# The first batch's attention product in plain float32, in a fused attention, SoLU and Mish kernel on one core

## The chip, the cores and the metric

The kernel runs on one core of a Trainium2 chip. The metric is the device time of one execution in microseconds (us). The kernel before was run three times; one more number counts here, the span of the profiled execution, which is the time from its first to its last instruction.

## What is computed

The reference is an attention block followed by two feed-forward blocks over 2304 tokens. It is cut here to what matters.

```python
# x: (4, 8, 512, 64), state: (4, 8, 32, 64), all float32
a     = softmax(x @ state^T / sqrt(64));   xread = a @ state      # 512 tokens per batch
a2    = softmax(state @ x^T / sqrt(64));   sread = a2 @ x         # 32 tokens per batch
t     = concat(xread, sread)  ->  (2304, 512)
h     = t @ w_in                                  # 512 x 1024
solu  = h * softmax(h)
ln    = (solu - mean) / sqrt(var + 1e-6) * g_ln
y     = ln @ w_out                                # 1024 x 512
h2    = y @ w2_in                                 # 512 x 2048
out   = (h2 * tanh(softplus(h2))) @ w2_out        # 2048 x 512
```

## The kernel before

**Stages.** The 2304 tokens lie in 17 tiles of 128 rows: four tiles for each batch's 512 tokens and one tile for the state tokens of all batches. The first stage makes the attention weights, the hidden layer `h` of each tile, its SoLU and layer norm, and the product with the first output matrix. The second stage runs over three passes of 6, 6 and 5 tiles and multiplies with the second block's matrices by a scheme with seven products in place of eight (the products are on line 860, their sums on lines 871 to 882, the activation on lines 894 and 901). Pass 0 also splits and stores the second block's weights, which passes 1 and 2 fetch again.

**Attention merged with the first matrix.** The kernel doesn't form `xread`. It multiplies the state with `w_in` first (lines 493 and 504), which gives merged weights `sw` with 128 rows (four heads of 32 states) for each half `q` of the heads, and then `h` of a tile is the transposed attention weights `aT` times `sw`, summed over the two halves (line 530, `s_a0`).

**Split products.** A factor is kept as a rounded part `hi` in the type F32R and a rest `lo`, and one product is three matmuls: hi*hi, hi*lo and lo*hi. For the attention weights `weights_of` makes the two parts (ScalarE casts on line 346, VectorE subtracts on line 348), for the merged weights `split_sw` does (lines 486 and 488). A flag per batch, `A`, takes another way through the same functions, which the kernel before has off for all four batches:

```python
def weights_of(b, q, src):
    both = aTp.tile([P, 2, S], F32R, tag="aT", name="aT")
    if eng('A', b, False, True):
        (nc.scalar.copy if eng('C', 2 * b + q, ...) else nc.vector.tensor_copy)(out=f32(both[:, 0]), in_=src)
        aT[b, q] = f32(both[:, 0]); return
    hi, lo = both[:, 0], both[:, 1]
    nc.scalar.copy(out=hi, in_=src)                                             # line 346
    nc.vector.tensor_tensor(out=lo, in0=src, in1=f32(hi), op=ALU.subtract)      # line 348

def s_a0(i):
    for q in range(2):
        terms = ((aT[b, q], f32(sw(b)[0])),) if eng('A', b, False, True) \
                else ((ah, wh), (ah, wl), (al, wh))
        for k, (a_, w_) in enumerate(terms):
            for hf in range(2):                                                 # two halves of 512 columns
                nc.tensor.matmul(out=ph[:, hf*512:(hf+1)*512], lhsT=a_[:, c*P:(c+1)*P],
                                 rhs=w_[:, q, hf*512:(hf+1)*512], ...)          # line 530
```

**A tile's chain.** After `s_a0` the steps of `s_a1` follow: VectorE takes the maximum (line 539), ScalarE the exponential (542), VectorE the product with `h` (544), ScalarE the squares (548), GpSimd some small steps, and ScalarE or VectorE the norm (559 or 562). The accumulator `ph` of a tile is a PSUM tile of a pool with two slots, which the products for `sw` use too. Its last reader is line 548. So tile k+2 can't start before line 548 of tile k has run. Then the normed tile is transposed on TensorE (575) or by VectorE and DMA (586 to 595), split in two parts (579 and 581, or 597 and 599), and multiplied with the output matrix (616).

**What sets the order.** The order of issue on all engines is one table, `ORDER`: each two letters name a step of the program, and every naming issues the step's next piece. Strings of flags, `FLAGS`, choose the engine for single operations: `M` for the copy on line 871 and `S` for that on line 921 (ScalarE or VectorE), `P` for the subtraction on line 599 (VectorE or GpSimd), `B`, `W` and `T` for the steps that make float32 out of the 64-bit inputs (lines 149 to 165), `N`, `Q` and `Z` for small ones. Each engine runs its own instructions in the order of issue.

Of the kernel before, what the change touches and what calls it, by code (L numbers as in the profile page):

```python
# [19 lines left out]
B, H, S, NS, D = 4, 8, 512, 32, 64  # L20
DM, FF1, FF2 = 512, 1024, 2048
NTOK = B * (S + NS)
P = 128
# [48 lines left out]
    "AAAABGBGATBIBIBKBKAUAUARARAWAWBABAA0A0BHBHA-A-ATBHBHA6A6BJABABBJBPAQAQBJBOANANAYAYBLBJAJAJA2A2BLBCBCBPADADAaAaBO"  # L72
    "BRAFAFBQBRBXA8A8BBBLBBBUBBAVAVBLBXBXA1APAPBTAXAXA1BQA1BUBBA4A4AOAOBTBSAZAZA_A_BeA7A_A7BSBUBEBEA1A7BhBhA_AbAbA3Bg"
    "BgBDBDASASB5BDBeBeA7B5AcAcBUBUA3B5B7AeAeA9BDB6B7AgAgB5B7BVBiBiB6B7B8A3AiAiBVB6A5A9A5A9A5BbBbAdAdA3BVBYBYA9AfAfA5"
    "B8BfBfBFBFBaBaBVBjBZBZBFB5BjB8BVBVBVBnAhAhB6BcB7AjAjBFB6BWB6B8BdBcBWBkBkBnBWBMBqBnBdAkAkBlB8AmAmB_BNCJAoAoBdBoAq"
# [1131 lines left out]
```

## Time and profile before

| | |
|---|---|
| median of 3 runs (lowest to highest) | 576.29 us (575.89 to 576.59) |
| the profiled execution's own time | 576.29 us |
| its span | 574.6 us |
| TensorE (PE) busy | 558.4 us (97%) |
| VectorE (DVE) busy | 500.2 us (87%) |
| ScalarE (ACT) busy | 364.2 us (63%) |
| GpSimd (POOL) busy | 54.5 us (9%) |
| granted TensorE clock | 1.000 of 2.4 GHz |

The profiled execution took the median's time, and 1.7 us of it lie outside the span. Busy time is a share of the whole span; the stages differ, so the rows further down are read by stretch. A PE row's duration runs on after the next matmul has begun, so the price of a matmul is the distance from its start to the next one's start.

### The profile page before, as it was taken

To read this page: it belongs to the slowest core of one execution; us is meant where nothing else is said; L and a number is where in the kernel's file an instruction comes from. 1 tells how busy PE (TensorE), PEld (TensorE's weight loads), DVE (VectorE), ACT (ScalarE), POOL (GpSimd) and SP (SyncE) were. 2 spreads that over 40 slices of the span, in tenths; PEclk is the share of its full clock that TensorE was granted. 3 is DMA by queue.
4 is the path that set the end of the run, shared out by engine and by line. 5 is a ranking of instruction groups with operands and counts; after the bars stand their busy time and mean duration, and the time that the engine had idled before them with its cause. 6 is when DMAs were issued, how large, how long until landed. Compare 5 with 4: busy or idle time off the path is not lost. (4 is left out here: it accounts for less than half of the span.)

```text
span 574.6 us, 9808 instructions
## 1 busy us (share of the span) xinstructions
PE 558.4 (97%) x3557; PEld 497.6 (87%) x3557; DVE 500.2 (87%) x949; ACT 364.2 (63%) x659; POOL 54.5 (9%) x134
## 2 busy tenths in 40 slices
PE   9977999999999999999999999999999999999997
PEld 3435787899789998888988989999999999999996
DVE  5999988896668878999999996689889998889996
ACT  5997968656458956999998774542433636433340
POOL 0102212210023000000000000000000024000024
PEclk9999999999999999999999999999999999999999
DMA  8952205123206688899988699876866779888832
GB/s 345 414 200 94 74 38 165 57 75 111 74 38 220 204 292 277 307 348 391 342 312 292 249 337 320 312 264 231 327 204 250 255 263 333 302 293 332 293 144 92
DMA packets 47279, 136.04 MB, mean 237 GB/s; under 512 B 5376, under 2 KB 20864, under 8 KB 46720
## 3 DMA queue, kind: packets, MB, share of 16 engines
q1 hardware_dynamic: 47232, 135.42, 66.3%
q8 instruction: 28, 0.46, 0.3%
q14 instruction: 19, 0.16, 0.1%
HBM read 96.60 MB, written 38.80 MB: 236 GB/s over the span
## 5 line engine op out<-in xcount | busy, mean ns | idle before, releaser
L860 PE MATMUL hp<-xo,w2r 128*128 128x384 f32 (+1 forms) x504 | 94.3, 328 | 0.1
L860 PEld LDWEIGHTS hp<-xo,w2r 128*128 128x128 f32 x504 | 84.8, 188 | 3.1 <-DVE u L874 0.4
L860 PE MATMUL hp<-xo,w2swh 128*128 128x384 f32 (+1 forms) x336 | 83.3, 331 | 2.0 <-DVE c L882 0.5
L616 PE MATMUL pm<-ln_l,gw_hi 128*128 128x256 f32 (+1 forms) x256 | 77.6, 303 | 0.6 <-ACT raw_c L621 0.5
L616 PE MATMUL pm<-ln_h,gw_hi 128*128 128x256 f32 (+1 forms) x256 | 74.9, 293 | 0.0
L616 PE MATMUL pm<-ln_h,gw_lo 128*128 128x256 f32 (+1 forms) x256 | 74.5, 291 | 0.0
L972 DVE TENSOR_TENSOR acc<-po,acc 128x384 f32<-128x384 f32 (+1 forms) x136 | 68.4, 521 | 3.6 <-PE po L967 3.1
L860 PEld LDWEIGHTS hp<-xo,w2swh 128*128 128x128 f32 x336 | 59.1, 188 | 6.2 <-DVE c L882 1.6
L901 ACT ACTIVATE gh<-c 128x384 fp32r<-128x384 f32 (+1 forms) x57 | 29.2, 519 | 53.2 <-DVE c L882 47.8
L860 PE MATMUL hp<-xo,w2swl 128*128 128x384 f32 (+1 forms) x168 | 55.0, 328 | 0.0
L616 PEld LDWEIGHTS pm<-ln_l,gw_hi 128*128 128x128 f32 x256 | 48.3, 189 | 4.5 <-DVE ln_l L581 1.1
L939 ACT CAST qh<-t 128x384 fp32r<-128x384 f32 (+1 forms) x60 | 28.4, 489 | 35.6 <-DVE t L931 18.0
L882 DVE TENSOR_TENSOR c<-hp,u 128x384 f32<-128x384 f32 (+1 forms) x72 | 38.0, 532 | 13.4 <-PE hp L860 12.9
L616 PEld LDWEIGHTS pm<-ln_h,gw_hi 128*128 128x128 f32 x256 | 48.2, 188 | 1.2 <-issue 0.7
L616 PEld LDWEIGHTS pm<-ln_h,gw_lo 128*128 128x128 f32 x256 | 48.6, 190 | 0.0
L530 PE MATMUL ph<-swh,aT 128*128 128x512 f32 x128 | 40.5, 405 | 3.8 <-ACT ph L548 2.5
L965 PE MATMUL po<-ql,w2oh 128*128 128x384 f32 (+1 forms) x120 | 39.5, 330 | 0.2 <-DVE acc L972 0.2
L966 PE MATMUL po<-qh,w2oh 128*128 128x384 f32 (+1 forms) x120 | 38.8, 324 | 0.0
L967 PE MATMUL po<-qh,w2ol 128*128 128x384 f32 (+1 forms) x120 | 38.8, 323 | 0.0
L159 ACT CAST w<-w 128x512 f16<-128x512 f32 x22 | 30.7, 1394 | 3.2 <-DVE w L156 2.8
L941 DVE TENSOR_TENSOR ql<-t,qh 128x384 fp32r<-128x384 f32 (+1 forms) x60 | 30.9, 533 | 1.1 <-ACT qh L939 0.6
L860 PEld LDWEIGHTS hp<-xo,w2swl 128*128 128x128 f32 x168 | 31.5, 188 | 0.0
(454 smaller groups left out, 1355.2 us busy)
## 6 DMA issues: line engine op xcount, KB each, us to landing
w2r<-ki SPq DMA_DIRECT2D x16, 768.0 KB, 6.1
w2ol<-ko SPq DMA_DIRECT2D x15, 768.0 KB, 6.3
w2oh<-ko SPq DMA_DIRECT2D x15, 768.0 KB, 6.0
w<-in_w2i SPq DMA_DIRECT2D x16, 512.0 KB, 5.4
w2swl<-ki SPq DMA_DIRECT2D x8, 896.0 KB, 6.7
w2swh<-ki SPq DMA_DIRECT2D x8, 896.0 KB, 7.5
w<-in_w2o SPq DMA_DIRECT2D x12, 512.0 KB, 5.5
ki<-w2r SPq DMA_DIRECT2D x8, 768.0 KB, 8.8
```

What stands on the lines that cost most here:

```text
L159: nc.scalar.copy(out=src.bitcast(F16)[..., 1], in_=f32(high))
L530: nc.tensor.matmul(out=ph[:, hf * 512:(hf + 1) * 512], lhsT=a_[:, c * P:(c + 1) * P], rhs=w_[:, q, hf * 512:(hf + 1) * 512], start=q == 0 ...
L616: nc.tensor.matmul(out=pm[:, :n], lhsT=w_[:, k, m * P:(m + 1) * P], rhs=l_[:, c0:c0 + 4 * len(blk), k, :], start=k == 0 and j == 0, stop=k ...
L860: nc.tensor.matmul(out=r, lhsT=w_[:, 0, k * P:(k + 1) * P], rhs=x_[:, k, :n], start=s in (0, 1, 3, 4) and cnt == 0, stop=cnt == 5, skip_gr ...
L882: nc.vector.tensor_tensor(out=c, in0=bank[ps, fp, s], in1=u, op=ALU.add)
L901: nc.scalar.activation(out=gh, in_=src, func=AF.Mish)
L939: nc.scalar.copy(out=hi, in_=src)
L941: on('V', ((ps - 1) * NFP + fp) * 4 + int(name[1]) - 1).tensor_tensor(out=lo, in0=src, in1=f32(hi), op=ALU.subtract)
L965: nc.tensor.matmul(out=r, lhsT=wh[:, a, c], rhs=x[1], start=first or not held, stop=False)
L966: nc.tensor.matmul(out=r, lhsT=wh[:, a, c], rhs=x[0], start=False, stop=False)
L967: nc.tensor.matmul(out=r, lhsT=wl[:, a, c], rhs=x[0], start=False, stop=last or not held)
L972: on.tensor_tensor(out=o, in0=x, in1=y, op=ALU.add)
```

## The change

It turns flag `A` on for batch 0, so that its attention weights and merged weights are kept in plain float32 in one part each, and each product of its four tiles is one plain matmul in place of three. `C` puts the two copies of the attention weights on ScalarE and those of the merged weights (a new line in the profile, 483) on VectorE. `ORDER` is a new table, and flags of other steps change with it. No function changes.

```diff
 FLAGS = dict(
-    A="0000",
-    B="0000011100011000010010111010",
-    C="000000000000",
+    A="1000",
+    B="0000111100011000010110111101",
+    C="110000000000",
...
-    M="001100001110000000000010",
-    N="00010001110010001",
+    M="001001111010000000010100",
+    N="01000010100101001",
-    P="00000000000000000",
-    Q="111011111111110101010001",
+    P="00000100000000000",
+    Q="111110101100110101010001",
-    S="000110",
+    S="111001",
-    W="1101010100000001111000000000",
-    X="00111010001100100101010001000101",
+    W="1101010100000011111010000000",
+    X="10101000101110010000110001010001",
-    Z="11101011110011101",
+    Z="11100101011001100",
...
-    "P2QGP3QFQHQFPzP4QJQGQHQGP0QIQHQKQIQIQJQKQJQK"
+    "QHQFP0P4QGQIQHQGPzQHQJQIQKQIQJQKQJQK"
```

Over the whole program the instructions that change in number are: on PE line 530 from 192 matmuls to 160 (48 split ones less, 16 plain ones more); on DVE line 348 from 8 to 6, line 488 from 8 to 6, line 483 from 0 to 2, line 599 from 9 to 8 (one goes to POOL), line 871 from 6 to 8, line 921 from 2 to 4; on ACT line 346 from 8 to 6, line 341 from 0 to 2, line 486 from 8 to 6, line 871 from 18 to 16, line 921 from 4 to 2; and a few of the short steps on lines 149 to 165 and 422 to 546 go from one engine to another.

The first place is PE from the first tile of batch 0 to the second. In the names, `ph` with the lowest number is tile 0's accumulator, the next one tile 1's; `aT` are the attention weights of the two halves, `swh` and `swl` the merged weights, and the `tr` rows are transposes for batch 1's and batch 0's softmax. Before:

```order
L465 MATMUL tr_477<-ident_58,srs_436 128x128
L530 MATMUL ph_484<-swh_389,aT_444 128x512 x2
L530 MATMUL ph_484<-swl_390,aT_444 128x512 x2
L530 MATMUL ph_484<-swh_389,aT_444 128x512 x2
L334 MATMUL tr_501<-ident_58,tt_475 128x128 x4
L530 MATMUL ph_484<-swh_389,aT_471 128x512 x2
L530 MATMUL ph_484<-swl_390,aT_471 128x512 x2
L530 MATMUL ph_484<-swh_389,aT_471 128x512 x2
L334 MATMUL tr_523<-ident_58,tt_494 128x128 x4
L530 MATMUL ph_530<-swh_389,aT_444 128x512 x2
```

And now:

```order
L465 MATMUL tr_473<-ident_58,srs_455 128x128
L530 MATMUL ph_475<-swh_404,aT_427 128x512 x2
L334 MATMUL tr_495<-ident_58,tt_484 128x128 x4
L530 MATMUL ph_475<-swh_404,aT_469 128x512 x2
L334 MATMUL tr_515<-ident_58,e2_506 128x128 x4
L530 MATMUL ph_520<-swh_404,aT_427 128x512 x2
L334 MATMUL tr_532<-ident_58,tt_488 128x128 x4
L530 MATMUL ph_520<-swh_404,aT_469 128x512 x2
L334 MATMUL tr_546<-ident_58,e2_511 128x128 x4
L334 MATMUL tr_552<-ident_58,tt_484 128x128 x4
```

Each half of a tile is now one pair of matmuls, and the transpose for batch 1's other half (`tt_494` before, `tt_488` now) stands behind the first half of tile 1, no longer ahead of tile 1.

The second place is DVE ahead of the first tile's maximum (line 539). `swl_457` before and `swl_442` now are batch 1's merged weights, whose second products `ph_461` and `ph_446` hold the slot that tile 1 needs. Before:

```order
L488 TENSOR_TENSOR swl_390<-ph_370,swh_389 128x1024
L348 TENSOR_TENSOR aT_444<-tr_428,aT_444 128x512
L488 TENSOR_TENSOR swl_457<-ph_408,swh_456 128x2x512
L420 TENSOR_REDUCE m2_481<-st_447 128x1
L348 TENSOR_TENSOR aT_471<-tr_438,aT_471 128x512
L420 TENSOR_REDUCE m2_499<-st_446 128x1
L295 SCALAR_TENSOR_TENSOR gw_lo_131<-wo64_291,g_t_59,gw_hi_130 128x512 x2
L385 TENSOR_REDUCE mx_520<-tr_501 128x16
L488 TENSOR_TENSOR swl_457<-ph_461,swh_456 128x2x512
```

And now:

```order
L483 COPY swh_404<-ph_371 128x1024
L431 RECIPROCAL s2_354<-s2_354 128x1
L295 SCALAR_TENSOR_TENSOR gw_lo_131<-wo64_279,g_t_59,gw_hi_130 128x512
L488 TENSOR_TENSOR swl_442<-ph_416,swh_441 128x2x512
L295 SCALAR_TENSOR_TENSOR gw_lo_131<-wo64_279,g_t_59,gw_hi_130 128x512
L420 TENSOR_REDUCE m2_482<-st_460 128x1
L420 TENSOR_REDUCE m2_490<-st_459 128x1
L488 TENSOR_TENSOR swl_442<-ph_446,swh_441 128x2x512
L385 TENSOR_REDUCE mx_509<-tr_495 128x16
```

The subtractions for `aT` are gone, a copy stands in the place of the subtraction for `sw`, and batch 1's second subtraction has moved ahead of line 385.

The third place is ACT from the transposed weights of batch 1 to tile 0's squares (line 548). Now:

```order
L438 COPY a2_526<-tr_515 128x512
L542 ACTIVATE ez_530,lnsm_523<-ph_475,lnsm_523 128x1024
L389 ACTIVATE tt_488<-tt_488 128x512
L346 CAST aT_567<-tr_552 128x512
L548 ACTIVATE ph_475,lnsm_523<-ez_530,lnsm_523 128x1024
```

This piece reads the same before with other numbers: line 548 of tile 0 stands behind line 346, and line 346 waits for a transpose that PE runs, now as before, behind all of tile 1.

## Rows read from the trace of the kernel before

**Rows 1.** Windows view: stretch, length, busy us of each engine, TensorE clock, DMA share, GB/s.

```profile
core 0: us, PE busy (x) PEld busy (x) DVE busy (x) ACT busy (x) POOL busy (x), PEclk, DMA share, GB/s
40.00:50.00 10.00, 8.70 (x57) 6.44 (x57) 9.86 (x17) 7.45 (x17) 1.07 (x3) 1.00 0.33 108
50.00:60.00 10.00, 6.95 (x74) 4.61 (x59) 9.93 (x16) 8.38 (x15) 4.50 (x17) 1.00 0.31 105
60.00:70.00 10.00, 9.59 (x96) 7.07 (x94) 9.92 (x21) 9.94 (x19) 2.70 (x10) 1.00 0.34 107
70.00:110.00 40.00, 40.00 (x357) 32.36 (x350) 34.10 (x47) 27.81 (x47) 8.88 (x28) 1.00 0.27 93
202.00:330.00 128.00, 125.93 (x640) 112.93 (x639) 120.03 (x256) 110.25 (x189) 0.00 (x0) 1.00 0.87 311
330.00:571.00 241.00, 240.71 (x1453) 234.81 (x1451) 210.56 (x440) 107.42 (x241) 19.95 (x20) 1.00 0.76 270
```

**Rows 2.** Timeline of PE, 40 to 68 us: start, us, instruction, idle time before it and releaser.

```profile
40.97 0.73 PE L530 MATMUL ph<-swh,aT 128*128 128x512 f32 x2 [0.38 <-DVE swl L488]
...
45.81 0.73 PE L530 MATMUL ph<-swh,aT 128*128 128x512 f32 x2 [0.92 <-DVE swl L488]
...
53.45 0.73 PE L530 MATMUL ph<-swh,aT 128*128 128x512 f32 x2 [2.06 <-ACT ph L548]
...
58.09 0.65 PE L452 MATMUL sr<-xn_t,a 128*32 128x64 f32 x32 [0.82 <-DVE tt L381]
...
59.71 1.07 PE L530 MATMUL ph<-swh,aT 128*128 128x512 f32 x4
60.62 0.62 PE L530 MATMUL ph<-swl,aT 128*128 128x512 f32 x2
...
63.70 0.73 PE L530 MATMUL ph<-swh,aT 128*128 128x512 f32 x2 [0.41 <-ACT ph L548]
...
67.56 0.37 PE L616 MATMUL pm<-ln_l,gw_hi 128*128 128x256 f32 x1
```

**Rows 3.** Timeline of PE at the plain float32 products of the state tile.

```profile
156.14 2.74 PE L517 MATMUL ph<-w_in_t,xs 128*128 128x512 f32 x6
158.71 1.02 PE L517 MATMUL ph<-w_in,xs 128*128 128x512 f32 x2
159.17 0.68 PE L616 MATMUL pm<-ln_l,gw_hi 128*128 128x256 f32 x1
159.69 0.28 PE L616 MATMUL pm<-ln_h,gw_hi 128*128 128x256 f32 x1
```

**Rows 4.** Lines view, by form: count, busy us, mean ns of one, idle time before.

```profile
L488 DVE TENSOR_TENSOR swl<-ph,swh 128x1024 fp32r<-128x1024 f32 x8 | 9.7, 1209 | 1.2 <-ACT swh L486 1.2
L486 ACT CAST swh<-ph 128x1024 fp32r<-128x1024 f32 x8 | 8.4, 1054 | 1.7 <-PE ph L504 1.7
L348 DVE TENSOR_TENSOR aT<-tr,aT 128x512 fp32r<-128x512 f32 x4 | 2.7, 683 | 0.0
L599 DVE TENSOR_TENSOR ln_l<-ln_l,ln_h 128x1024 fp32r<-128x1024 f32 x9 | 10.9, 1220 | 2.8 <-ACT ln_h L597 2.8
L871 DVE COPY m<-hp 128x384 f32<-128x384 f32 x5 | 2.8, 551 | 0.0
L972 POOL TENSOR_TENSOR acc<-acc,acc 128x320 f32<-128x320 f32 (+1 forms) x10 | 10.2, 1027 | 4.8 <-DVE acc L972 4.8
```

**Rows 5.** Timeline of DVE, 39 to 48 us.

```profile
39.70 1.21 DVE L488 TENSOR_TENSOR swl<-ph,swh 128x1024 fp32r<-128x1024 f32 x1
...
44.55 1.21 DVE L488 TENSOR_TENSOR swl<-ph,swh 128x1024 fp32r<-128x1024 f32 x1
...
46.28 1.21 DVE L539 TENSOR_REDUCE lnsm<-ph 128x1 f32<-128x1024 f32 x1
```

**Rows 6.** Timeline of ACT, 51 to 63 us.

```profile
51.44 0.59 ACT L346 CAST aT<-tr 128x512 fp32r<-128x512 f32 x1 [0.97 <-PE tr L334]
52.16 1.12 ACT L548 ACTIVATE ph<-ez,lnsm 128x1024 f32<-128x1024 f32 x1
...
62.41 1.11 ACT L548 ACTIVATE ph<-ez,lnsm 128x1024 f32<-128x1024 f32 x1
```

More of the change, by code (lines that the diff above doesn't have):

```diff
@@ new lines @@
+    "BaBaB8A9BFBbBbBFBfBfBVBVBFBVB8B5BjBWB6AhAhBFBqAjAjBWBcB6BNBdB6BqB7BNBnB8BqBMBkBkBdBMBnB8CJB8AkAkB_BlAmAmBoB9B_Ao"
+    "AoBlBnAqAqCJCJB9B9BlB_BlB-CNCKBlB-BlCKBoBlBlBlCNCNBoBoCKCABoBmBrBrBmBoCKCKCKBmBoB9COAsAsCRCKAuAuCBCOAwAwCKCDAyAy"
+    "CBCRCRCKCOCBBoBoCOCLCOCOBsCSCBB-B-CLCOCOCVCABsCSBsCDCAB9B_CLCDCVCVB_CSAlAlBsCDAnAnCAApApCOArArCMCSCSCSBpCWBpCZCS"
+    "CWBpCSBsCPCSCWCZCZCPCMCPCBCWCaDFCWCWCQBsDFBsCaBsCWBuCDCMCQBvCWCCCWCQDHBvDFBuCaDHCCDHCaBuCaCaDFBvBxCaBvDFCTBvCaCA"
+    "CcCTBvBvCaCTBvCcCcCABxCbCEBxCbDGDHCdCYDHDGCdCfCYCdCfCfCYCdCdCdDGCgDGCdCCCCCgDGCdCiCECgCdCXCiCiCgCgCgCeDECXCjCgCg"
@@ new lines @@
+    "CeB1CXCjCECgDEAtAtB1CjDEAvAvAxAxCEDEAzAzChCjDJCjCjCeCeDJBtCeDECjCUCeBtB1B4CbCUCjChCjCbCUDKCbBtDJCbB4BwDJBwB4DKDJ"
+    "CeCECmBwCECeCmCmDKCnDKCqCnDKCnCbCqCqCnCbCnCnByByCrCkCtCnCnCFCrCnCFCtCtCFBzCFCrClDLCuDLCrCrCrDLB2DLCuCHCrCwB2CrDL"
+    "BzCrBzDICuBzDIDICkB2CuDICuCuBzCwCwChDIClCsChCuB2ChDMCuChCkCuCsDMCxDMCHClCpCHDMBzBzCxBzCHDODMB0ChDOCxCIB0DOB0DOB2"
+    "CIDNCvB2DNDODNCvChDPCxCFDPB2CxCxB2DNCHDPCxCxDNDSCxDSCyDSCyDSDPDSCICsDPCpCGCsB3DTCsCsCpB3DTB3DTCGDTCoDTCGCGCoDQCo"
+    "CIDQCsDRCsDQDRDQDRDQCIDkDkDlDlDlDRCIDoCzCyDRCyDqDoCyCyDqDoDoCzCvCvDpCvCvCzDqDqDpDpDpCyCzCzCyDWC0CvDWDWC0CvDVC0DV"
@@ new lines @@
+    "DWC0DVDWC0C0C2C0C2C2C0C0DVC3C5DVC1C3DXC1C3C5C5C3DUC3C3C6DUDUC6C3C3C9C3C6C9C9C4C6C6C6DXC-C4DUC6DXDUC-C6DXDAC6C1C-"
+    "C1C1DXDADAC1C-C-C-C4C4C4DaDrDmC-C4DaDBDrDYC-DaDrDrC-DaDmDmC1C8C_DvDwC7DBDYC1C_DYDaDsC4DZDBDvDZDvDZC4DvDZDBDYDBDB"
+    "DZDvDbDYDBDBDbD3DwD8D8D3DbC7DwDbEAEADsDwDeDsDwC_C_DeDxD5C_DxDbDxDeC_DxDxD4D9D9DBDdDsD4DdD5D6DtDdC7C8EBEBDdD-D-Ds"
+    "C_DCD6DeDdDyEGC8DzDcECECDeC_DcDtDfDyDzDcDtDtDfDtDfDuDCDuD0DcDuDuDuD1DfD0DcD1D2DDDCEHDDD7D7DhDDDfD2DhEGEDEGDhD_D_"
+    "EGEHDiEHEGDhEHEOETETEODiDhEHEXEXDiEIEQEIEIEUEUDjEIEIEPEDEREPDiEVEVEQEEEDDjEYEYDiEREDEaDjEZEZEDDjEJEKESEJDgEKEWDj"
@@ new lines @@
+    "DgEEDgEEEEEEDgEFELEFEFDgEFEFELEeE0EdGkGkGmDnGmGnDnDnENGmEMGnEMGmGoENESESEaEbEaExGnEWEWGoEaGoGmEeEeGtGtGnEeEaGmE0"
+    "GrE0GmGmGnGrEeE0GsGsGnGnGrGuGuGqE0GqG4GpGqEnEdG4GpEdErErEnG5E8GzGzEvEvG5EdFBFBGpG0G0E8GwGwEhEbEbFFFFEdG4EgEfEbEf"
+    "GyGyExExG6GvGvEbElGxGxEcG6EqEqEcEiG2G2EcFLEcEcEjG4ElEkEfEuEuG3G3EkEmEpEpExG6G4G5EiG1G1G5EyEmHAHAG9FMG9EjG4EfEfG9"
+    "E1EoG4G4G5EsEsFLG8G_G_FLG5G5EgG-G-G7EoG8HKEhFLEwEwG8FIHKEtEtHLG7FLEyHFHFG7EyHLHKEyExHGHGHMEyHMHKE3HMFMFAE3HCHCE4"
+    "HLFEE1HKE4EzFTEzE5EzHKFYFYE1HLEzEzE6HEHEE5E7E6HDHDE1FAFAE7FJHKHKFMFfHLFMFEFEE1HJHJHLHLHIHIE-FMHOFCFCHcE2HPE-HPHQ"
@@ new lines @@
+    "HQFNHdFGFGE2HOHRHRFIFIFNHBHBE2FIFNHHHHE2E2FiFNFNE9HcFjFIFUHOFVHcHdFPFZFZFUE_HSHSFJHPFDFDHWHWE_FfFPHcHNE9FWI2HNFH"
+    "FHHXHXHeFaFaHNHYHYHeFWFfHUHUHdFeFeFfI2HVHVHeHcFVFiFJFiF5HcFdFdHdFJFfHTHTHdFiFJHkHkFKFjHZHZFKFOFKHcHcFKFKFRI2FQHj"
+    "HjFjHdHdFRHaHaHfFSFOHbHbFiFgFjHuFXFXFSFTHgHiHiHhI2FcFcHvFjHuF6HhFQHgHhF2HuFmHgFbFbFqHfFvFvFqHqHqFlHfF5FzFzHoHoI2"
+    "FuHwHnHnFsFkHvHlHlF5FsHwHuFwFwFkF5HwF0F0HuFkHvFgFkFkHtHtHvFtI2HuHzI2HzFtFgH2H2HzFrGQHuHuHvFgFxFxFlFrHmHmHyFmHpHp"
+    "HyGRFgF6FyH0H0HvHvF1F1F6FhHsHsFhHxF5IAHxF6I2I2FhH1H1IBFoHyHrHrFnFoH8H8GBHxIAF2FhFhGGGGF6F3F2H4H4GBF2FnH5H5GKGKIB"
```

87 lines of the change are left out of this document (31 added, 56 removed).

## The prediction

> **What bounds the kernel now.** I read the windows view first. From 70 us on PE is busy in every stretch to within 0.1 us, but for 202 to 330 us, where 2.07 of 128 are idle; from 330 to 571 it is 0.29 of 241 [rows 1]. So after 70 us the time is PE's work, and another engine counts there only where it makes PE wait. From 40 to 70 us it is the other way round: PE idles 1.30, 3.05 and 0.41 us in the three windows of 10 us, while DVE is busy 9.86, 9.93 and 9.92 of each [rows 1]. The timeline of PE shows what it waits for there: between the first matmul of tile 0 at 40.97 us and that of tile 4 at 63.70 lie waits of 0.92, 2.06, 0.82 and 0.41 us, 4.21 in all, ended by DVE's second subtraction for batch 1's merged weights, by ACT's squares (line 548, which free an accumulator slot) and by a DVE transpose [rows 2]. The four tiles of batch 0, which the change touches, run just in this stretch. Whether dearer products cost time is thus a question of how much of them falls into these waits.
>
> **What PE has to do more.** A split matmul of 512 columns takes 0.228 us (four of them from 59.71 to 60.62 [rows 2]), so the three of one product take 0.68. The plain product has its like in the state tile: line 517 issues four products there as eight records, from 156.14 us to 159.17, and the matmul behind them is held 0.40 us more (it lasts 0.68 where its successor lasts 0.28): 3.43 us, or 0.86 for each; the first six records alone give the same, 2.57 over three [rows 3]. Sixteen products (four tiles, two halves of the heads, two halves of the columns) make 16 x (0.86 - 0.68) = **2.8 us more on PE**, 0.70 for each tile. The Trainium skill would make it worse: its page "FP8 and Floating Point Precision", section "TensorE Precision Notes", has four passes for true FP32, and "TensorE: Matmul & The Clock Gate", section "Back-to-back issue gap", a gap of about 216 ns for 512 columns; my estimate from both is 16 x 0.216 = 3.5 us, by which the forecast below would be 0.7 higher. The trace bears out the four passes (0.86 is four times 0.215), but not 216 ns for a split matmul with its own weight load (228), and the rows decide.
>
> **What DVE and ACT have to do less.** DVE loses the two subtractions on line 348, 0.68 each, so 1.4 us. The two on line 488 become copies of the same shape out of PSUM; such a copy doesn't stand in the trace. Its bounds are a gain of 0.16 us (ACT's cast of the shape, 1.05) and a loss of 0.3 (the 0.55 of DVE's 384-column copy scaled by width gives 1.47); I take no change, since the subtraction of the very shape takes 1.21 [rows 4]. ACT loses the two casts on line 486, 2.1 us; the casts on line 346 become copies and stay. One subtraction on line 599, 1.22 us, leaves DVE for POOL, where I scale line 972 by width to 3.3 us [rows 4]; POOL is busy 8.88 of 40 us from 70 to 110 [rows 1], which hides it, and a late one would cost 2.1. The short steps that go between engines on lines 149 to 165 are 0.4 to 0.6 us each on both, go both ways, and I cost them at nothing up to 70 us.
>
> **The front, step by step.** I follow the change's order with the durations of the trace.
> - Tile 0 waits for the slot that a subtraction for batch 1's merged weights frees, at 40.91 us before [rows 5]. One subtraction less stands ahead of it, but ACT's cast ahead of it stands behind a product with `g` that DVE supplies late. I take no gain: 41.0.
> - Tile 1's slot is freed by the subtraction that started at 44.55 [rows 5]. It now stands ahead of line 385 and without a line 348, so it ends near 43.9 and the wait of 0.92 goes. But PE has tile 0 until 45.5 and a transpose until 46.1, so tile 1 starts at 46.1 against 45.81.
> - Tile 0's maximum waited in DVE's queue until 46.28 [rows 5]; it now starts at 45.65. That lead is lost again at line 548, which stands behind line 346, which waits for a transpose behind all of tile 1 (0.97 us before [rows 6]). Tile 1, longer by 0.70, ends at 50.2, the transposes at 51.4, the cast at 51.95, and tile 0's squares start there against 52.16 [rows 6]. Tile 2: 53.15 against 53.45 [rows 2].
> - The same goes once more round: tile 2's squares come at 62.7 against 62.41 [rows 6], and tile 4 starts at 63.9 against 63.70.
> - Line 616, which began at 67.56 [rows 2], needs a subtraction behind tile 3's product on DVE; I get 67.8, with one group of transposes (0.55) less done by then. PE is 0.8 us behind where it was.
>
> So of the 2.8 us about 2.0 fall into waits, and **0.8 remain**. The bounds: if all 4.21 us of waits could take them, nothing would remain and DVE's lead would count; if each tile's chain took its 0.70 in full, 2.8 would.
>
> **After the front.** From 70 to 202 us PE is full, so 0.8 stays 0.8. In pass 0 (202 to 330 us) DVE is busy 120.03 of 128, ACT 110.25, and PE waits 2.07 [rows 1]. DVE comes to it with 2.6 us less done on the way (1.4 of line 348, 1.2 of line 599), ACT with 2.1 less, and PE 0.8 later, so the waits at its start should shrink. Within the pass DVE gets more: two copies of line 871 at 0.55 and two of line 921, which I price by line 348's 0.68, in all 2.5 [rows 4]. Of the 2.07 I take half, **-1.0**; the ends are -2.1 and +2.5. From 330 us on there is nothing to gain, and the changed flags there only trade one copy for another.
>
> **The sum.** The profiled execution took 576.29 us, which is the median too: 576.29 + 0.8 - 1.0 = **576.1 us**. A difference under 0.2%, 1.15 us, is about what a measurement of this kernel can't tell from none; so the forecast is no change.
>
> **The rivals.**
> - *DVE's amount of work sets the front*, not the chain between the engines. For it: DVE's 9.9 of 10 us [rows 1]. Against it: the waits named in rows 2 and 6 end with one engine's late result, not with a backlog. Then the 1.4 us of line 348 come through whole, and nothing of the 2.8 shows: 576.3 - 1.4 = 574.9. Chance 0.19.
> - *Pass 0 loses its waits.* For it: DVE's and ACT's lead of over 2 us, more than the 2.07 that PE idles. Against it: DVE has more to do inside the pass. With the 0.8 kept and 2.1 won: 575.0, or less where waits go that hide in stretched matmuls. Chance 0.18.
> - *Pass 0 becomes DVE's.* Place: 202 to 330 us; the 2.5 us of copies lie on an engine that is busy 94% there. It decides once DVE, at 122.5 of 128, is the last releaser of the products on line 860 and of line 917's inputs for most of the pass. Price: the 2.5, with the 0.8 of the front absorbed in them: 578.8. Chance 0.15.
> - *The plain product lies on the path whole*, because two slots bind each tile to the squares two tiles back, so that the 0.70 of each tile follow one another: 576.3 + 2.8 = 579.1. Against it: the maxima wait in DVE's queue 1 us and more after PE is done. Chance 0.10.
>
> That the change isn't what it says has no chance of its own: the order of issue shows one pair of matmuls for each half of a tile.
>
> **The numbers.** The forecast has 0.38. Faster by over 0.2% are the first two rivals, 0.37; within 0.2% is the forecast, 0.38; slower are the last two, 0.25. The range from 574.0 to 578.9 holds the forecast, both faster rivals but for a front and a pass 0 that both gain, and the first slower one; most of the last is left out.
>
> **What would show it.** Right: line 530 with 160 split records and 32 plain ones, the plain ones 0.43 us apart; tile 4 starting at 63.4 to 64.4 us; PE idle under 2.5 us between tile 0 and tile 4; the first line 616 at 67.5 to 68.5; from there to 200 us no idle PE; then under 2 us of PE waits in pass 0. Wrong: a plain record that isn't 0.43 us; tile 4 before 63 us (the first rival) or after 65 (the last); more than 3 us of idle PE in pass 0, with DVE as the releaser (the third).

## The result, and the profile after

The changed kernel took 581.08 us (median of 6 runs, 580.94 to 582.40), the kernel before 576.44 on the same chip (575.49 to 577.13). The ratio is 1.0086, with a 95% interval of 1.0076 to 1.0097: slower by 4.6 us, where no change was forecast and the range ended at 578.9.

Three points of the program tell where it went, read off PE's timeline in the profiled executions. "Tile 0" is the first line 530, "616" the first line 616, "pass 0" the first line 860; all in us.

| | tile 0 | 616 | pass 0 | end of span | 616 to pass 0 | pass 0 to end |
|---|---|---|---|---|---|---|
| before | 40.97 | 67.56 | 221.62 | 574.59 | 154.06 | 352.97 |
| forecast, step by step | 41.0 | 67.8 | 0.8 late | 0.2 early | 0.55 more | 1.0 less |
| after | 43.23 | 70.44 | 226.46 | 579.38 | 156.02 | 352.92 |

So 2.26 are lost before the first of the dearer products has begun, 0.6 between there and the first line 616, 2.0 between line 616 and pass 0, and nothing after it. Of the 2.0, about 0.4 are a group of transposes (line 575) that the new order runs behind the first line 616 and the old one ahead of it; the forecast had the group, at 0.55. The other 1.6 are idle time: PE idles 2.24 us of this stretch, where the kernel before idles 0.63.

The windows view of after; columns as in [rows 1], with two earlier windows that were not read before. Behind it stand three single lines: the kernel before from 20 to 30 us, and the first 108 us from the first line 860 on, before and after.

```profile
core 0: us, PE busy (x) PEld busy (x) DVE busy (x) ACT busy (x) POOL busy (x), PEclk, DMA share, GB/s
20.00:30.00 10.00, 7.91 (x37) 4.01 (x35) 7.71 (x15) 7.80 (x11) 3.30 (x3) 0.88 1.03 409
30.00:40.00 10.00, 9.00 (x70) 4.86 (x66) 9.79 (x14) 8.61 (x12) 0.21 (x1) 0.95 0.48 162
40.00:50.00 10.00, 9.26 (x59) 4.30 (x59) 8.85 (x13) 8.30 (x19) 0.42 (x2) 1.00 0.36 108
50.00:60.00 10.00, 7.92 (x40) 3.43 (x39) 9.78 (x19) 7.21 (x13) 3.25 (x12) 1.00 0.33 105
60.00:70.00 10.00, 9.41 (x96) 5.87 (x96) 9.05 (x17) 8.78 (x19) 3.42 (x11) 1.00 0.33 107
70.00:110.00 40.00, 39.58 (x357) 32.75 (x357) 32.14 (x50) 28.84 (x48) 9.55 (x26) 1.00 0.28 93
202.00:330.00 128.00, 124.74 (x651) 113.35 (x650) 120.05 (x255) 108.33 (x184) 0.00 (x0) 1.00 0.89 320
330.00:571.00 241.00, 240.01 (x1444) 233.97 (x1443) 214.41 (x444) 109.18 (x244) 17.88 (x18) 1.00 0.75 268
```

```profile
20.00:30.00 10.00, 8.76 (x54) 4.42 (x52) 9.81 (x18) 9.93 (x14) 1.96 (x4) 1.00 1.03 409
```

```profile
221.60:330.00 108.40, 106.36 (x525) 93.57 (x524) 104.51 (x224) 99.63 (x172) 0.00 (x0) 1.00 0.88 317
```

```profile
226.46:334.80 108.34, 106.33 (x529) 94.71 (x529) 104.85 (x225) 100.75 (x174) 0.00 (x0) 1.00 0.91 325
```

Against [rows 1], PE is busier from 40 to 60 us: the dearer products do fill waits there. The window that doesn't fit is 20 to 30 us: DVE and ACT are busy only 7.7 and 7.8 of 10 us, where the kernel before has 9.81 and 9.93, and POOL is busy 3.30 with three instructions.

PE's timeline of after, the rows that answer to [rows 2], and some more.

```profile
28.23 1.11 PE L493 MATMUL ph<-w_in,bd_t 128*64 128x512 f32 x1 [2.02 <-DVE w_in L161]
...
40.78 1.09 PE L504 MATMUL ph<-w_in_t,st_t 64*32 64x512 f32 x16 [0.74 <-DVE s L431]
...
43.23 1.88 PE L530 MATMUL ph<-swh,aT 128*128 128x512 f32 x4
...
47.66 1.88 PE L530 MATMUL ph<-swh,aT 128*128 128x512 f32 x4
49.38 0.60 PE L334 MATMUL tr<-ident,tt 128*128 128x128 f32 x4
...
55.20 3.70 PE L530 MATMUL ph<-swh,aT 128*128 128x512 f32 x8 [0.97 <-ACT ph L548]
...
66.53 0.73 PE L530 MATMUL ph<-swh,aT 128*128 128x512 f32 x2 [0.50 <-ACT ph L548]
...
70.44 0.39 PE L616 MATMUL pm<-ln_l,gw_hi 128*128 128x256 f32 x1 [0.42 <-DVE ln_l L581]
...
71.27 0.60 PE L575 MATMUL tr<-ident,ez 128*128 128x128 f32 x4
71.63 0.37 PE L616 MATMUL pm<-ln_l,gw_hi 128*128 128x256 f32 x1
...
209.30 0.42 PE L616 MATMUL pm<-ln_l,gw_hi 128*128 128x384 f32 x1 [1.25 <-ACT ln_h L579]
```

The plain product costs what was forecast: two of them take 1.72 us (47.66 to 49.38), 0.86 each. Tile 2 still waits for ACT's squares (0.97 where it was 2.06), and from tile 0 to tile 4 it is 23.30 us against 22.73 before and 22.9 in the forecast: 0.6 of the 2.8 remain there, 0.4 more than I had. What is new is the wait of 2.02 us at 28.23, far ahead of tile 0, and that of 1.25 us at 209.30, where nothing was to wait.

The lines view of after answers to [rows 4]: line 483 takes as long as the subtraction that it replaces, as assumed, and the subtraction that went to POOL takes 2.39 us there, where I had scaled 3.3.

```profile
L488 DVE TENSOR_TENSOR swl<-ph,swh 128x1024 fp32r<-128x1024 f32 x6 | 7.3, 1210 | 0.3 <-ACT swh L486 0.3
L483 DVE COPY swh<-ph 128x1024 f32<-128x1024 f32 x2 | 2.4, 1206 | 0.0
L599 POOL TENSOR_TENSOR ln_l<-ln_l,ln_h 128x1024 fp32r<-128x1024 f32 x1 | 2.4, 2391 | 5.4 <-DMA ln_l<-td 5.4
```

**The wait at 28.23, followed back.** It ends with a half of `w_in` from DVE (line 161). The timelines of POOL, ACT and DVE, 21 to 28 us, in after:

```profile
21.82 2.87 POOL L422 TENSOR_SCALAR m<-m 128x1 f32<-128x1 f32 x1 [20.53 <-DVE m L420]
...
25.88 0.21 POOL L422 TENSOR_SCALAR m<-m 128x1 f32<-128x1 f32 x1
```

```profile
24.72 0.69 ACT L427 ACTIVATE e<-st,m 128x512 f32<-128x512 f32 x1 [2.16 <-POOL m L422]
...
26.10 2.52 ACT L159 CAST wi<-wi 128x512 f16<-128x512 f32 x2
```

```profile
21.64 0.74 DVE L295 SCALAR_TENSOR_TENSOR gw_lo<-wo,g_t,gw_hi 128x512 fp32r<-128x512 f32 x1
22.30 0.42 DVE L149 TENSOR_SCALAR wi<-wi 128x512 f32<-128x512 f32 x1
22.64 1.29 DVE L161 SCALAR_TENSOR_TENSOR w_in_t<-wi 128x512 uint32<-128x512 uint32 x2
23.84 0.42 DVE L149 TENSOR_SCALAR wi<-wi 128x512 f32<-128x512 f32 x1
24.18 0.42 DVE L156 TENSOR_SCALAR wi<-wi 128x512 uint32<-128x512 uint32 x1
24.51 0.69 DVE L420 TENSOR_REDUCE m<-st 128x1 f32<-128x512 f32 x1
27.48 0.69 DVE L161 SCALAR_TENSOR_TENSOR w_in<-wi 128x512 uint32<-128x512 uint32 x1 [2.29 <-ACT wi L159]
```

Line 422 scales a maximum, one number per partition, and both kernels run it on POOL. The second one takes 0.21 us; the first takes 2.87, and it ends (24.69) when DVE's six instructions on SBUF (two of them in the row of line 161) are over (24.60) and a reduction that reads PSUM has begun. ACT's exponential stands behind it, the cast of line 159 behind the exponential, DVE's line 161 behind the cast, PE's line 493 behind that. In the kernel before the same step took 0.94 us; its rows on POOL and DVE:

```profile
24.06 0.94 POOL L422 TENSOR_SCALAR m<-m 128x1 f32<-128x1 f32 x1 [22.77 <-DVE m L420]
```

```profile
23.84 0.73 DVE L161 SCALAR_TENSOR_TENSOR w_in_t<-wi 128x512 uint32<-128x512 uint32 x1
24.45 0.47 DVE L156 TENSOR_SCALAR wi<-wi 128x512 uint32<-128x512 uint32 x1
24.78 0.73 DVE L420 TENSOR_REDUCE m<-st 128x1 f32<-128x512 f32 x1
```

The change left the step on its engine; the new order put six SBUF instructions of DVE behind the maximum where two had stood.

### The profile page after: what moved, and what is told of

Its sections match the earlier page's. It is cut to its first block, busy times and chain, and to the rows that moved or that the text cites. A ratio compares the mean times of both kernels' runs of the same rounds, so it can differ in the third digit from the quotient of the medians.

```text
span 579.4 us, 9781 instructions
## 1 busy us (share of the span) xinstructions
PE 562.5 (97%) x3541; PEld 496.8 (86%) x3541; DVE 502.3 (87%) x955; ACT 361.2 (62%) x654; POOL 55.1 (10%) x129
## 5 line engine op out<-in xcount | busy, mean ns | idle before, releaser
L616 PE MATMUL pm<-ln_l,gw_hi 128*128 128x256 f32 (+1 forms) x256 | 76.3, 298 | 2.2 <-ACT ln_h L579 1.3
L530 PE MATMUL ph<-swh,aT 128*128 128x512 f32 x128 | 44.5, 450 | 1.5 <-ACT ph L548 1.5
```

Of the source, the lines that this page charges most:

```text
L530: nc.tensor.matmul(out=ph[:, hf * 512:(hf + 1) * 512], lhsT=a_[:, c * P:(c + 1) * P], rhs=w_[:, q, hf * 512:(hf + 1) * 512], start=q == 0 ...
L616: nc.tensor.matmul(out=pm[:, :n], lhsT=w_[:, k, m * P:(m + 1) * P], rhs=l_[:, c0:c0 + 4 * len(blk), k, :], start=k == 0 and j == 0, stop=k ...
```

## Experiments

18 kernels ran beside the kernel before, 4 to 12 executions each. "Over" is the median less the median of the kernel before on the same chip. The kernel before took 575.98 to 576.58 on the five chips, so runs are compared by "over" and not by the absolute times that the expectations name. The ratio is formed from the single executions; turned into us it differs from "over" by up to 0.6. The three columns on the right are read as in the table above, each from one profiled execution, which can lie off the median (by 1.2 us in i1, 1.7 in e2).

| | over, us | ratio, interval | 616 | 616 to pass 0 | pass 0 to end |
|---|---|---|---|---|---|
| after | 4.64 | 1.0086 (1.0076 to 1.0097) | 70.44 | 156.02 | 352.92 |
| e1 plain product, old order | 0.78 | 1.0009 (0.9998 to 1.0020) | 67.52 | 154.04 | 354.24 |
| e2 new order, split | 7.69 | 1.0134 (1.0114 to 1.0154) | 73.72 | 155.76 | 354.76 |
| e3 after, line 422 on DVE | 2.41 | 1.0036 (1.0023 to 1.0049) | 68.33 | 156.05 | 352.01 |
| e4 new flags, old order | 6.54 | 1.0107 (1.0090 to 1.0124) | 68.77 | 156.12 | 355.83 |
| f1 new order, old flags | 6.74 | 1.0117 (1.0104 to 1.0130) | 68.51 | 157.06 | 354.90 |
| f2 new front, old rest, new flags | 7.60 | 1.0132 (1.0119 to 1.0145) | 68.66 | 156.97 | 356.42 |
| f3 old front, new rest, new flags | 2.54 | 1.0047 (1.0032 to 1.0063) | 68.70 | 155.70 | 352.62 |
| f4 e1, line 422 on DVE | 0.79 | 1.0024 (1.0012 to 1.0037) | 68.89 | 153.61 | 352.82 |
| g1 e3 to pass 0, then old | 3.53 | 1.0062 (1.0050 to 1.0074) | 68.20 | 155.79 | 353.60 |
| g2 f4 to pass 0, then new | 1.16 | 1.0028 (1.0012 to 1.0044) | 67.64 | 154.04 | 353.73 |
| g3 before, line 422 on DVE | 1.99 | 1.0031 (1.0019 to 1.0043) | 67.47 | 154.04 | 354.96 |
| g4 e3, state tile moved on PE | 3.23 | 1.0051 (1.0039 to 1.0063) | 68.33 | 156.25 | 352.93 |
| h1 e3, state tile moved everywhere | 4.28 | 1.0075 (1.0063 to 1.0088) | 68.28 | 157.57 | 353.44 |
| h2 e3, batch 3's line 422 on DVE | 2.51 | 1.0039 (1.0025 to 1.0053) | 68.31 | 155.87 | 352.95 |
| h3 h1 and h2 | 4.52 | 1.0074 (1.0062 to 1.0087) | 68.38 | 156.94 | 353.50 |
| i1 new front, old rest, own flags | 2.91 | 1.0051 (1.0038 to 1.0063) | 68.62 | 155.82 | 354.02 |
| i2 old front, new rest, own flags | 1.09 | 1.0020 (1.0011 to 1.0028) | 67.62 | 155.23 | 352.79 |
| i3 after, one maximum earlier | 3.80 | 1.0063 (1.0049 to 1.0076) | 70.02 | 155.78 | 352.56 |

### Plain product or order?

e1 is the kernel before with the flags of the plain product alone.

```diff
-    A="0000",
+    A="1000",
-    C="000000000000",
+    C="110000000000",
```

> The order of issue and all other flags of the kernel before, with the first batch in plain float32 alone (the copies of its attention weights on ScalarE, of its merged weights on VectorE). Theory 1 (the loss is made by the new order, ahead of tile 0, and the plain products' 2.8 us of TensorE work fall mostly into waits of the front): tile 0 starts within 0.4 us of 40.97, tile 4 at 63.9 to 64.5, and the time is 577.2 us (576.6 to 577.8), that is 0.2 to 1.4 over the kernel before. Theory 2 (the plain products lie on the path whole): 2.8 over the kernel before, 579.2 (578.6 to 579.8), tile 4 near 66.5.

Measured: 0.78 us over the kernel before, and by the ratio 0.5, with an interval from -0.1 to 1.2. Theory 1 holds, but for tile 4, which starts at 63.21, earlier than either theory had it. e1's PE timeline:

```profile
40.70 1.98 PE L530 MATMUL ph<-swh,aT 128*128 128x512 f32 x4 [0.45 <-DVE swl L488]
...
53.08 3.70 PE L530 MATMUL ph<-swh,aT 128*128 128x512 f32 x8 [1.81 <-ACT ph L548]
...
67.52 0.37 PE L616 MATMUL pm<-ln_l,gw_hi 128*128 128x256 f32 x1
...
221.56 0.50 PE L860 MATMUL hp<-xo,w2swh 128*128 128x384 f32 x2
```

PE has 2.8 us more to do in the front and begins line 616 at 67.52 against 67.56: on the old order the waits take all of it. What e1 loses, it loses behind 221.56 us, where the program is the same as before.

e2 is the reverse: the changed kernel with the first batch split again, rounded part and rest made in one step.

```diff
-    A="1000",
+    A="0000",
...
         nc.scalar.copy(out=hi, in_=src)
-        yield
+        if b:
+            yield
```

> The order and the other flags of the changed kernel, with the first batch's products split as before (rounded part and rest are made one right behind the other). Theory 1 (the new order carries the loss): 580.3 us (579.6 to 581.0), tile 0 still starts after 42.5. Theory 2 (the plain products carry it): 581.1 less 2.8 = 578.3 (577.7 to 578.9).

Measured: 7.69 over, 3.1 more than after. Neither theory has it. Tile 0 starts at 46.86 there: PE waits 2.31 us for a subtraction that the plain product doesn't have, and then the granted clock falls, to a mean of 0.66 from 40 to 50 us (part of that window at 1.2 GHz). The new order is one for the plain product. So e2 brings losses of its own and can't separate product from order; it shows only that the new order isn't faster with the split product in it.

### GpSimd's step

e3 is after with line 422 of batch 0's first half on VectorE.

```diff
-    Q="111110101100110101010001",
+    Q="011110101100110101010001",
```

> The changed kernel with one 128x1 step (line 422 for the first half of batch 0) on VectorE; on GpSimd it took 2.87 us, from 21.82, and ScalarE stood 2.16 us behind it. Theory 1 (that step holds ScalarE's queue, with the cast for a w_in half behind it, and so tile 0): the idle 2.02 us of TensorE at 28.23 shrink below 0.6, tile 0 starts at 41.2 to 42.2 in place of 43.23, and the time is 579.1 us (578.6 to 580.0). Rival (the step is late but something else, the w_in halves' own loads or the VectorE queue, would hold tile 0 just as long): 581.1, within 0.5.

Measured: 2.41 over in place of 4.64; by the ratios the gain is 2.9 us. DVE does the step in 0.15 us. The wait ahead of line 493 is gone, and the front is near the forecast: tile 0 at 41.16 (41.0), line 616 at 68.33 (67.8). e3's PE timeline:

```profile
41.16 1.88 PE L530 MATMUL ph<-swh,aT 128*128 128x512 f32 x4
...
68.33 0.39 PE L616 MATMUL pm<-ln_l,gw_hi 128*128 128x256 f32 x1 [0.41 <-DVE ln_l L581]
```

i3 asks whether DVE makes the step long. It leaves line 422 on POOL and moves one DVE instruction, as the order of issue shows:

```diff
 L161 SCALAR_TENSOR_TENSOR w_in_t<-wi_175 128x512
+L420 TENSOR_REDUCE m_315<-st 128x1
 L149 TENSOR_SCALAR wi_175<-wi_175 128x512
 L156 TENSOR_SCALAR wi_175<-wi_175 128x512
-L420 TENSOR_REDUCE m_323<-st 128x1
```

> The changed kernel with one instruction moved on VectorE: the maximum of batch 0's second half (line 420, which reads PSUM) stands ahead of lines 149 and 156 (which read and write SBUF) in place of behind them; line 422 stays on GpSimd. If GpSimd waits for a gap in VectorE's work on SBUF: line 422 ends within 0.15 us of the end of the second line 161 of that run (23.93 in after), so it takes 2.1 to 2.3 us in place of 2.87. If its length is its own: 2.87. The time: between 0 and 0.7 below the changed kernel's 581.1, since the two moved steps then come 0.7 later.

The step takes 2.20 us, as expected. i3's timelines of POOL and of DVE:

```profile
22.04 2.20 POOL L422 TENSOR_SCALAR m<-m 128x1 f32<-128x1 f32 x1 [20.75 <-DVE m L420]
```

```profile
22.86 1.28 DVE L161 SCALAR_TENSOR_TENSOR w_in_t<-wi 128x512 uint32<-128x512 uint32 x2
24.07 0.68 DVE L420 TENSOR_REDUCE m<-st 128x1 f32<-128x512 f32 x1
```

It ends at 24.24, 0.10 behind the end of DVE's last SBUF instruction of that run (24.14) and before the reduction from PSUM has ended; ACT's exponential follows at 24.27, where after has 24.72. The time falls to 3.80 over, 0.8 below after, by the ratios 1.3, more than the 0.7 that I had allowed.

f4 and g3 move both of batch 0's steps of line 422 to DVE, on e1 and on the kernel before.

```diff
-    Q="111011111111110101010001",
+    Q="001011111111110101010001",
```

> e1 (the plain product on the old order and flags) with line 422's two steps for batch 0 on VectorE; on GpSimd they took 0.93 and 0.58 us there, ScalarE's exponential behind each, and TensorE idled 1.11 behind the first. If the front is bound by that chain: 0.4 to 0.9 less than e1, 576.5 to 577.0. If what is won in the front is lost again where pass 0 waits for weights from DMA: 577.4, as e1, within 0.4.

> The kernel before, with line 422's two steps for batch 0 on VectorE (0.94 and 0.59 us on GpSimd there). If that chain bounds the front and the front counts: 575.4 to 576.0. If another wait takes its place, or pass 0 swallows it: 576.4, within 0.4.

Neither gains: f4 is where e1 was, and g3 is 2.0 slower than the kernel before, where I had it equal or faster. In the old order POOL's 0.94 and 0.59 us are not what the front waits for: g3 reaches line 616 at 67.47 and pass 0 at 221.51, 0.1 earlier than before. (g3's and f4's profiles have a mean clock of 0.83 from 50 to 60 us; g2, with f4's front at 1.00, reaches line 616 at 67.64, where e1 has 67.52.) g3 loses its 2.0 behind pass 0, with every instruction there as before. That stretch took 352.8 to 355.0 us in the profiles of the five kernels that have the old rest with its own flags from there, besides the kernel before (e1, f4, g1, g3, i1). So a tenth of a microsecond ahead of pass 0 is no promise of the end.

### Order against flags, front against rest

e4 has the new flags on the old order; f1 and f2 mix in other ways, f3 joins the old front to the new rest.

```diff
-ORDER, flags M N P Q S W X Z B: old, old
+e4: old, new        f1: new, old, with e3's Q
+f2: new up to the first line 616 and old behind it, new flags, with e3's Q
+f3: old up to the first line 616 and new behind it, new flags, with e3's Q
```

> The kernel before with all the flags that the change turns besides the plain product (who scales, who copies, who subtracts), in the old order of issue. Theory 1 (the order, not the flags, makes the 1.9 us that are lost behind the front): 576.4 us (575.8 to 577.4). Rival (the flags make them): 577.8 to 578.8.

> The changed kernel's order with the plain product, line 422's first step on VectorE as in e3, and all other flags as before the change. Reference: e3, 578.99. Theory A (behind the front the flags carry the 1.6 us by which e3 is slower than e1): 577.4 (576.8 to 578.0). Theory B (the order carries them): 579.0 (578.4 to 579.6). Theory C (the flags and the order were chosen for each other, and a mixture loses as e4's did, 6.5): 581 or more.

> As e3 (all flags of the change, line 422's first step on VectorE), with the change's order up to the first product of line 616, and the old order of everything behind it. Theory B (the new order behind the front carries 1.6): 577.4 (576.8 to 578.2). Theory A: 579.0. Theory C (flags without their order): 581 or more, lost mostly between 70 and 330 us.

> The plain product with the old order up to the first product of line 616, the new order and the new flags behind it, line 422's first step on VectorE. The front is that of e1, where TensorE stood 0.4 us ahead of the kernel before at 200 us. If the front's order is worth nothing more once line 422 is mended: 579.0, as e3. If the new front still costs the 0.9 us by which e3 trails e1 at 66 us, and that comes through: 578.1. If pass 0 swallows whatever lateness there is: 577.4 to 579.0 with TensorE's idle time from 202 to 330 us over 3.

e4, f1 and f2 lose 6.5 to 7.6 us. Each queue's order was chosen for the engine that its flags give each step, and either with the other's partner is worse than both kernels; these three can't tell order from flags (my theory C). f3 lost 2.54, but its front has the new flags too. The next pairs cut the program once, order and flags together.

```diff
-ORDER and flags: old, old
+g1: e3's up to pass 0, old behind it          g2: f4's up to pass 0, new behind it
+i1: e3's up to the first line 616, old behind it
+i2: e1's up to the first line 616, new behind it
```

> e3 up to the first product of pass 0 (order and flags of the change, line 422's first step on VectorE), order and flags of the kernel before from there. Theory D (what the change still loses in e3, 2.5 over the kernel before, is lost ahead of pass 0, and pass 0 gives some of it back in either order): 578.5 to 579.5, as e3. Theory E (the new pass 0 and what follows lose it): 577.0 to 578.0. Theory F (TensorE comes 2 to 3 us later to an order made for an earlier one): 580 or more.

> f4 up to the first product of pass 0 (the plain product on the old order, both steps of line 422 on VectorE), order and flags of the change from there. Theory D: 577.2 (576.6 to 577.8), as f4. Theory E: 578.5 to 579.5. If the new pass 0 is the better one by the 1.8 us that e3 makes good there: 575.5 to 576.4.

> The change's order and flags up to the first product of line 616 (line 422's first step on VectorE, the plain product on), the order and the flags of the kernel before behind it. Theory: the new order with its own flags loses 2.0 us between the first product of line 616 and pass 0 (156.0 us in after and e3, 154.06 before), and the front, once line 422 is mended, costs the 0.8 that was forecast. Then the first product of line 616 starts at 68.2 to 68.5, pass 0 154.0 to 154.5 later, and the time is 0.8 over the kernel before (0.4 to 1.4), not the 2.4 of e3. Rival (the front sets up the loss behind it, so that it stays with the old rest): 2.0 to 2.8 over the kernel before, pass 0 155.5 or more after the first product of line 616.

> The old order and flags up to the first product of line 616 with the plain product on, as e1; the order and flags of the change behind it. Theory: first product of line 616 at 67.4 to 67.8, pass 0 155.5 to 156.3 later, and the time is 1.8 to 2.6 over the kernel before. Rival (the front sets up the loss): pass 0 154.0 to 154.5 later, and 0.8 over the kernel before, as e1.

g1 took 579.51 and g2 577.14, g2 as theory D has it and g1 at the upper end of D. Against its own kernel before g1 is 3.5 over, 1.1 more than e3, where D had them equal; so the old rest gives nothing back, and theory E is out. What e3 still loses is lost ahead of pass 0, and the new pass 0 is not the cause. i1 and i2 came out against me. With e1 and e3 they make a square:

| over, us | old rest | new rest |
|---|---|---|
| old front, plain product (e1, i2) | 0.8 | 1.1 |
| new front with line 422 mended (i1, e3) | 2.9 | 2.4 |

The new rest alone costs 0.3, which is within the intervals of e1 and i2, the mended new front 1.3 to 2.1. The rival that I set against my theory, that the front sets up the loss behind it, is the better reading. At the first line 616 the new front is 1.1 late with the same transposes done (i1 1.06; e3 0.77, and the group of 0.4 still to do), at pass 0 it is 2.8 late with either rest (224.38 and 224.44 against 221.62). How the front does it is not shown: in i1 PE's waits in that stretch are other ones than in after, of 0.5 us at most. The new rest loses 1.2 there even behind the old front (155.23 against 154.06); i2's profile has it back behind pass 0, by no more than the scatter of that stretch.

### Single waits of the stretch

The largest wait there is that at 207 to 209 us. Behind it ACT and DVE work on the second block's weights; ACT had waited 2.05 us for one of them from DMA, and line 579's casts and line 581's subtractions for the state tile stand in the same queues. g4 moves the last part of block 6's products behind the second transposes, and the state tile's first product ahead of the second cast; h1 moves the subtractions and the cast ahead of weight work too. The order of issue on DVE, h1 against e3:

```diff
 L657 TENSOR_TENSOR w_2066<-w_2203 128x256
+L581 TENSOR_TENSOR ln_l<-tr,ln_h 128x4x128
 L657 TENSOR_TENSOR w_2203<-w_2066,w_2203 128x256
 L657 TENSOR_TENSOR w_2066<-w_2066 128x256
 L657 TENSOR_TENSOR w_2203<-w_2066 128x256
+L581 TENSOR_TENSOR ln_l<-tr,ln_h 128x4x128
 L683 TENSOR_TENSOR w2swl<-w_2203,w2swh 128x256
 L683 TENSOR_TENSOR w2swl<-w_2066,w2swh 128x512
-L581 TENSOR_TENSOR ln_l<-tr,ln_h 128x4x128 x2
```

> e3 with three entries of the order moved: the second transposes of the state tile stand ahead of the last third of the products for block 6, and block 7's first products ahead of the second cast (line 579), as in the old order. TensorE's wait of 1.00 us for that cast at 207.22 should go in either case. If it comes through to the end: 578.0 (577.5 to 578.5). If pass 0, which waits for its weights from DMA, swallows it: 579.0 (578.6 to 579.5).

> e3 with the state tile's last steps moved ahead of weight work: both subtractions of line 581 ahead of the sums and subtractions of the second block's weights on VectorE (lines 657 and 683), the second cast of line 579 two places earlier on ScalarE, the second transposes ahead of the last third of block 6's products on TensorE. g4 moved the products and the cast alone, and the wait stayed 1.41, so I now hold VectorE's subtraction, queued behind the weights, for what ends it. Expected: the wait at 207 us falls from 1.00 to below 0.4. If that reaches the end: 578.0 (577.5 to 578.5). If pass 0 swallows it: 579.0 (578.6 to 579.4).

PE's timelines of g4 and of h1:

```profile
207.42 0.42 PE L616 MATMUL pm<-ln_l,gw_hi 128*128 128x384 f32 x1 [1.41 <-ACT ln_h L579]
```

```profile
208.00 0.44 PE L616 MATMUL pm<-ln_l,gw_hi 128*128 128x384 f32 x1 [0.95 <-ACT raw_d L621]
```

Both miss. In g4 the wait stayed and grew (1.41). In h1 it is 0.95 long and ends with another instruction: ACT's copy of a finished accumulator (line 621) now stands behind the moved cast. h1 is 1.9 slower than e3.

h2 takes the step of line 422 for batch 3 off POOL, in the chain of the wait at 114.75 us; h3 is h1 and h2.

```diff
-    Q="011110101100110101010001",
+    Q="011110001100110101010001",
```

> e3 with line 422's step for the first half of batch 3 on VectorE too; on GpSimd it took 0.72 us at 112.32, in place of 0.21, and TensorE waited 0.47 at 114.75 behind the chain it stands in. Expected: that wait falls below 0.15. If it reaches the end: 578.5; if it is swallowed or another wait takes its place: 579.0 (578.6 to 579.4).

> h1 and h2 together. If the waits between 66 us and pass 0 carry the 1.7 and it reaches the end: 577.5 (577.0 to 578.0), near f4's 577.2. If pass 0 swallows what is won ahead of it: 579.0.

h2's DVE timeline shows why the wait stayed (0.51):

```profile
112.10 0.80 DVE L562 TENSOR_SCALAR ez<-ez,lnsm 128x1024 f32<-128x1024 f32 x1
112.82 0.15 DVE L422 TENSOR_SCALAR m<-m 128x1 f32<-128x1 f32 x1
```

On POOL the step waited for line 562 to end (in e3 it ends at 113.04, line 562 at 112.96); in DVE's queue it stands behind the same line 562, and DVE's line 381 behind ACT's exponential starts at 113.87 in place of 113.89. h2's 578.52 is the time that I had named for a gain, by chance: against its own kernel before it is 2.51 over, e3 2.41. h3 lies with h1. Which piece of the new order carries the rest of the loss is not settled, and no version that I found is faster than the kernel before.

## Why the prediction was wrong

Of the 4.6 us, 0.8 come with the plain product (e1; its interval reaches zero), 2.2 to 2.9 with line 422's step (after less e3), and the 1.6 left (e3 less e1) with the new order, its front above all.

- **"Tile 0: I take no gain: 41.0" failed first.** I started the walk at tile 0 and took what lies ahead for unchanged but for two terms. It came at 43.23 by line 422, which the change neither moved to another engine nor made larger; with that one step on VectorE it comes at 41.16 (e3). I had costed the short steps of lines 149 to 165 at nothing by their length, line 422 doesn't stand in the prediction at all, and the trace of before had the sign in it: a 0.21-us step that took 0.94.
- **"0.8 remain" of the front was 0.3 to 0.4 short.** With line 422 mended, line 616 starts at 68.33 against the 67.8 of the walk. The 0.55 for the transposes still to do is borne out by no run: the group takes 0.36 in after (71.27 to 71.63) and 0.41 in the kernel before. So 1.1 to 1.2 remain in place of 0.8. The other terms hold: 0.86 for a product, the copies at the subtraction's 1.21, a smaller wait at tile 2, most of the 2.8 gone in waits. PE idles 2.67 us between tile 0 and tile 4 in after, where I had asked for under 2.5. On the old order nothing remains (e1). (After has 144 split and 32 plain records of line 530; my "160 split records" counted the 16 plain products in.)
- **"From 70 to 202 us PE is full, so 0.8 stays 0.8" failed.** It was read from a kernel whose PE idled hardly at all there, and that is a property of its order. In the new order the stretch from line 616 to pass 0 is 2.0 longer, 1.6 without the transposes, all of it idle PE, and its longest wait is the 1.25 us at 209.30. Being full said that there was no slack to win, not that a new order would keep it full.
- **"-1.0 in pass 0" was not what it was said to be.** From pass 0 to the end after takes 352.92 us against 352.97. The window from 202 to 330 us has 3.26 us of idle PE in after, over the 3 that I had named as wrong, but 1.25 of them are the wait at 209.30, ahead of pass 0. Counted from the first line 860 on, over the same 108 us of the program, PE idles 2.0 in both kernels: none of the waits was won. In e1, which has ACT's lead and 1.4 of DVE's 2.6, the stretch from pass 0 to the end took 1.3 more, in f4 0.15 less: the lead is worth nothing that can be told from this stretch's own scatter.
- **The rivals.** "Whole on the path" gave 579.1 for the plain product on whatever order; e1 measured 577.4. "DVE's work sets the front" gave 574.9; e1's front is 0.04 ahead of the kernel before, not 1.4. The third rival's two lines of copies can't be its cause either, as g2, which has them, is 0.4 slower than f4, less than the intervals. No rival held what happened, since none looked ahead of tile 0.

The forecast also took the change apart into the plain product, priced with care, and "order of issue chosen anew", walked along one chain. The second part decided.

## What to carry to other kernels

Price a new order of issue from the first instruction that moved, not from the place that the change is about, and look for short steps on GpSimd in a chain: what VectorE runs beside them is part of their price. A table of order and a set of engine choices belong together; with either alone this kernel lost 6 to 8 us. Extra work on an engine that waits can cost little (of 2.8 us at most 1.2 came through on the old order), but that is shown by changing that work alone.

## What the hardware showed that was not expected

**A GpSimd step can last as long as VectorE's run on SBUF.** The same 128x1 step took 0.21, 0.94, 2.20 and 2.87 us, and in the three longer cases it ended 0.1 us behind DVE's last SBUF instruction of a run. The Trainium skill has it: its page "GPSIMD Engine Reference", section "Specifications", says that GpSimd's SBUF interfaces are shared with VectorE and contended by VectorE instructions in a two-port mode or with two SBUF inputs. The trace agrees, and adds that a back-to-back run of six instructions left no gap for the step at all. Not every VectorE instruction on SBUF holds it: in after a POOL step of the same size took 0.19 us inside line 392, a reduction of an SBUF tile. So i3 doesn't tell whether the maximum let the step through because it reads PSUM or because it is a reduction. POOL's and DVE's rows of after:

```profile
53.95 0.19 POOL L550 TENSOR_SCALAR lnsm<-lnsm 128x1 f32<-128x1 f32 x1
```

```profile
53.50 0.68 DVE L392 TENSOR_REDUCE sm<-tt 128x16 f32<-128x512 f32 x1
```


**The clock can fall in one execution and not in another with the same instructions.** f4 and g2 have the same instructions up to pass 0. In f4's profile the mean granted clock is 0.83 of 2.4 GHz from 50 to 60 us (part of the window at 1.2 GHz), in g2's 1.00; eight plain records, after the same wait of 1.81 us, take 5.40 us in the one and 3.70 in the other, and the first line 616 starts at 68.89 and 67.64. The rows of f4 and of g2:

```profile
53.17 5.40 PE L530 MATMUL ph<-swh,aT 128*128 128x512 f32 x8 [1.81 <-ACT ph L548]
```

```profile
53.20 3.70 PE L530 MATMUL ph<-swh,aT 128*128 128x512 f32 x8 [1.81 <-ACT ph L548]
```

After's own profile has 0.88 and 0.95 from 20 to 40 us; another execution of it at a mean clock of 1.000 took 580.98 us, so the clock isn't its loss. Nor does it make tile 0 late: from the end of line 422's step to tile 0 it is 18.54 us in after and 18.59 in i3 (24.24 to 42.83), whose clock is 1.00 there.
